# A fused cosine attention and gated MLP on one core: attention visits of three events in three rotating PSUM slots, AV of a quad in one burst, and inverse norms by Newton steps on VectorE

## The chip, the core and the metric

The kernel runs on one core of a Trainium2 chip. The metric is the device time of one execution in microseconds (us); lower is better. The engines are named as in the profile: PE is TensorE (matmul), PEld its weight loads, ACT is ScalarE, DVE is VectorE, POOL is GpSimd, SP is SyncE, which here only issues transfers.

## The reference

```python
q_n = q / (norm(q, axis=-1) + 1e-6)          # q, k, v: 8 batches, 12 heads, 448 tokens, 64 wide
k_n = k / (norm(k, axis=-1) + 1e-6)
scores = q_n @ k_n.T / tau                   # tau = 0.1
attn = exp(scores - max);  attn = attn / (sum(attn) + 1e-9)
x = (attn @ v), heads side by side           # 3584 tokens x 768
h = x @ w_in                                 # 768 x 2048
g = h * cos(h)
out = g @ w_out                              # 2048 x 768
```

## The kernel before

Four heads of one batch are a **quad**; there are 24 quads (three per batch), numbered 0 to 23. A quad's keys come in NJ = 7 blocks of 64. One block's **score event** (`scores`, L551) is four matmuls of 64*64 quarters of the array into two neighbouring PSUM banks, and one ACT exponential E (L567) of 128x896 that empties them. One block's **AV event** (`attend`, L570) is four 64*64 matmuls that add E times V into banks X and Y (4 and 5); after seven of them DVE copies the pair to `AVs` (L586).

The sums of the exponentials are taken by `sums` (L630) for rounds of quads, [3], [4,5], [6,7] and so on: 28 matmuls with a 0/1 matrix into a spare bank, ACT's logarithm and exponential (L649, L651), a small store to DRAM from ACT's queue (L652), four loads from there that spread the reciprocals over the partitions (R, L658, on SP's queue), and a product `xT = AVs * R` on POOL (L662; for quad 5 on DVE).

The inverse norms of a quad come from `inverse` (L461). POOL squares Q and K (L450), DVE sums each 64 (L454), ACT takes logarithm and exponential for the root (L480, L483). For quads up to 7 DVE adds 1e-6 (L486) and takes the reciprocal (L489); from quad 8 two more ACT instructions do that (L491, L493). POOL then scales Q and K (L501), and SP's queue transposes them (`turn`, L539).

The MLP runs by batch c = 0 to 7. **M1** (L670 to L696) is 96 matmuls of 128x448 in eight pairs of banks, and for each pair ACT, DVE, ACT, DVE in turn (L689, L691, L693, L695) make g. **M2** (`m2`, L698) is 96 matmuls of 128x384 for even c and 128 for odd c, 16 to an item, in banks 6 and 7 in turn; DVE copies a finished item out (L722). A few last f blocks of the first two items are put off, since they need the last pairs of g.

The first three quads run alone. After that each batch c is a stage: M1, then M2 with attention of later quads between its matmuls. `QUADS` gives the quads per stage: 5, 4, 3, 3, 3, 3, 0, 0. In a stage `group` is the unit: one score, the AV events of the group before, one more score (groups of 2, 2, 2 and 1 blocks per quad), and then `fill` of some M2 matmuls. Score events use two pairs of banks in turn (0,1 and 2,3). A group is a change of PE from whole-array matmuls to quarter-array ones and back; I call it a **visit**. The AVs of a stage's last group run inside the next M1 (`flush_av`, L739).

All instructions of an engine are put in order by `Planner` (L22), which plays the kernel through with estimated durations; PE keeps the order written down, the other engines take what is ready and most urgent, where `lead` makes an instruction more urgent by so many us. On the chip each engine then works strictly in that order and waits on semaphores. A DVE or ACT instruction that needs the result of an earlier one of its own engine waits for it by semaphore as well.

Of the kernel before, what the change touches and what calls it, by code (L numbers as in the profile page):

```python
# [271 lines left out]
def bass_cosine_attention__then__act_gcu_kernel(  # L272
# [31 lines left out]
    NE, NV, NA = 17, 4, 4  # L304
# [17 lines left out]
    Zs = ring("Zs", 2, [128, S], F32)  # L322
# [105 lines left out]
    H, NLEAD, FAST = 2 * NJ, 5.0, 7  # L428
# [31 lines left out]

    def inverse(qd, w0, w1, part=ALL[0], after=()):  # L461
# [17 lines left out]
        lead = NLEAD * (qd > FIRST + 1)  # L479
        act("exp", 0.12, lambda e: e.activation(z, t, ACT.Ln, bias=1e-30, scale=1.0), r=cells("n2"), w=cells("nrm"),  # L480
            after=after, lead=lead)
# [3 lines left out]
        if 0 < qd <= FAST:  # L485
            op("dve", 0.13, lambda e: e.tensor_reduce(out=o, in_=both, axis=AX.X, op=ALU.add), r=cells("nrm") + ["eps"],  # L486
               w=cells("rr"), lead=lead)
            yield
            op("dve", 0.27, lambda e: e.reciprocal(o, o), r=cells("rr"), w=cells("rr"), lead=lead)  # L489
# [61 lines left out]
    def scores(g):  # L551
# [3 lines left out]
        u, bs, es = qd % 2, 2 * (g % 2), g % NE  # L555
# [14 lines left out]
    def attend(g):  # L570
# [13 lines left out]
        if j == NJ - 1 and qd >= FIRST:  # L584
            sl = qd % NA
            op("dve", 1.01, lambda e: e.tensor_copy(AVs[sl].ap(), two(X)), r=pair(X), w=[("AV", sl)])  # L586

    Z, LEAD = 6, 15.0

    def spread(qd, j0, j1):  # L590
# [14 lines left out]
        if j1 < NJ:  # L605
            return
        summed.add(qd)
        act("exp", 0.815, lambda e: e.activation(ar[s].ap(), two(Z), ACT.Ln, bias=0.0, scale=1.0), r=pair(Z), w=[("ar", s)])
        act("exp", 0.83, lambda e: e.activation(ar[s].ap(), ar[s].ap(), ACT.Exp, bias=0.0, scale=-1.0),  # L609
            r=[("ar", s)], w=[("ar", s)])  # L610

    def scale_x(qd):
        b, c0, s = qd // QB, 2 * (qd % QB), qd % 3
        op("dve", 1.01, lambda e: e.tensor_tensor(xT[b % 2].ap()[:, c0:c0 + 2, :], two(X), ar[s].ap(), ALU.mult),
           r=pair(X) + [("ar", s)], w=[("x", b % 2, qd % QB)])
# [12 lines left out]
    rounds, spared = [0], []  # L628

    def sums(quads, bk):  # L630
# [3 lines left out]
        z = n % 2  # L634
# [3 lines left out]
        def mm(e):  # L638
# [9 lines left out]
        zz = Zs[z].ap()[0:32 * np_, :]  # L648
        act("exp", 0.44, lambda e: e.activation(zz, bank(bk, S, 0, 32 * np_), ACT.Ln, bias=0.0, scale=1.0),  # L649
            r=whole(bk), w=[("Zs", z)], lead=LEAD)  # L650
        act("exp", 0.47, lambda e: e.activation(zz, zz, ACT.Exp, bias=0.0, scale=-1.0), r=[("Zs", z)], w=[("Zs", z)], lead=LEAD)  # L651
        op("act", 0.6, lambda e: e.dma_start(rscr.ap()[8 * n:8 * n + rows, :], Zs[z].ap()[0:32 * np_:16, :]),  # L652
           r=[("Zs", z)], w=[("rs", n)], dma=("rs", z), moves=0.05, lead=LEAD)
        for i, qd in enumerate(quads):
            u, sl, b = qd % 2, qd % NA, qd // QB
            for r in range(2):
# [5 lines left out]
            op("dve" if late else "pool", 1.02 if late else 2.04, lambda e, u=u, sl=sl, b=b, c0=c0: e.tensor_tensor(  # L662
                xT[b % 2].ap()[:, c0:c0 + 2, :], AVs[sl].ap(), R[u].ap(), ALU.mult),
                r=[("AV", sl), ("R", u, 0), ("R", u, 1)], w=[("x", b % 2, qd % QB)], lead=LEAD)
# [18 lines left out]
    def m1(c, pr, bk):  # L683
        s = pairs[0] % 3
        pairs[0] += 1
        col = S * (c % 2)
        bs = pair(bk)

        op("act", 0.815, lambda e: e.activation(ar[s].ap().bitcast(I32), two(bk), ACT.Identity, bias=0.25, scale=INV2PI),  # L689
           r=bs, w=[("ar", s)])  # L690
        op("dve", 1.005, lambda e: e.scalar_tensor_tensor(ar[s].ap(), ar[s].ap().bitcast(I32), -2.0 * math.pi, two(bk),  # L691
                                                          ALU.mult, ALU.add), r=bs + [("ar", s)], w=[("ar", s)])
        act("sin", 0.86, lambda e: e.activation(ar[s].ap(), ar[s].ap(), ACT.Sin, bias=GUARD * math.pi / 2.0, scale=GUARD),  # L693
            r=[("ar", s)], w=[("ar", s)])
        op("dve", 1.01, lambda e: e.tensor_tensor(gT.ap()[:, 2 * pr:2 * pr + 2, col:col + S], two(bk), ar[s].ap(), ALU.mult),  # L695
           r=bs + [("ar", s)], w=[("g", c % 2, 2 * pr), ("g", c % 2, 2 * pr + 1)])  # L696
# [35 lines left out]
    W, MOST = (1, 1), 9  # L732
    ROUNDS = [[FIRST]] + [[i, i + 1] for i in range(FIRST + 1, NQ, 2)]
    E1, E2 = NNB - 6, NNB - 4
    due = []
    last_group = []
    cur = [7]

    def flush_av():  # L739
        while last_group:  # L740
            g = last_group.pop(0)
            attend(g)
            qd, j = divmod(g, NJ)
            if j == NJ - 1 and NV <= qd + NV < NQ:
                load_v(qd + NV)

    def now():
        return [[o for o in P.ops if o.eng == "pe"][-1]]
# [5 lines left out]
    def group(steps):  # L754
        qd, j = divmod(steps[0], NJ)
        if j == 0:
            begin(qd)
        scores(steps[0])
        flush_av()
        for g in steps[1:]:  # L760
            scores(g)
        last_group.extend(steps)
        if FIRST < qd < NQ - 3 and j == 0:
            norm_a(qd + 3, [o for o in P.ops if o.eng == "dve"][-1:])
        if qd + 2 < NQ and j == NJ - 1:
            turn(qd + 2)
            if FIRST < qd < NQ - 4:
                load_qk(qd + 4)
        if j == 0:
            due.extend(r for r in ROUNDS if r[-1] == qd - 1)  # L770

    def groups_of(qd):
        g = NJ * qd
        return [range(g + i, g + min(i + 2, NJ)) for i in range(0, NJ, 2)]
# [141 lines left out]
    done = FIRST  # L916
    for c in range(B):
        last = 2 * ((NJ * done - 1) % 2)
        free = 2 - last
        if c == 0:  # L920
            at_bank = free, last, 6, X, free, 6, last, X
        elif c < B - 1:
            at_bank = free, 6, last, X, 6, free, last, X
        else:
            at_bank = 2 * (6, free, last, X)
        banks = (6, 7, free) if c >= B - 2 else (6, 7)
# [4 lines left out]
        for pr in range(NNB // 2):  # L931
            m1_part(c, pr, at_bank[pr], order if pr < early else (0, 1), late if pr < early else 0, NKC)
            m1(c, pr, at_bank[pr])
            if pr == 1:
                flush_av()
        if c == 0:
            transpose(FIRST, 0, free)
            transpose(FIRST, 1, free + 1)
# [6 lines left out]
        cuts = (0, E1, E2, E2 + 2, NNB)  # L945
        ahead = 2 if len(banks) == 2 else 3
        items[0:ahead * NNB] = [(*work[i], f) for a, b in zip(cuts, cuts[1:]) for i in range(ahead) for f in range(a, b)]
        at = [0]
        bank_of = {}

        def fill(n):
            n = min(n, len(items) - at[0])
            while n > 0:
                t, h, f0 = items[at[0]]
                if len(banks) == 3:
                    if due and at[0] >= E1:
                        sums(due.pop(0), free + 1)
                elif due and len(bank_of) != 1 and at[0] >= 2 * NNB and 2 <= f0 <= 13:
                    sums(due.pop(0), 13 - cur[0])
                f1 = f0  # L960
                while n > 0 and f1 < NNB and items[at[0]:at[0] + 1] == [(t, h, f1)]:
# [3 lines left out]
                    if due and f1 == 2:  # L965
# [5 lines left out]

        new = done + QUADS[c]
        todo = [steps for qd in range(done, new) for steps in groups_of(qd)]
        more = new > done
        done = new
        if todo:
            fill(2 * (E2 if c else E1))
        for i, steps in enumerate(todo):
            if c == 0 and i == 1:
                spared.extend([x([o for o in P.ops if o.eng == "dve"][-1:]) for x in adds])  # L980
                norm_b(FIRST + 2, after=[o for o in P.ops if o.chain][-1:])
            group(steps)
            left = len(items) - at[0]
            share = [W[len(x) & 1] for x in todo[i:]]
            fill(2 * (NNB - E2) + 3 * len(due) if i == 0 else min(MOST, -(-left * share[0] // sum(share))))
        if more and done == NQ:
            flush_av()
            due.extend(r for r in ROUNDS if r[-1] == NQ - 1)
# [37 lines left out]
```

## Time and profile before

| what | value |
|---|---|
| median of 3 runs | 441.71 us (440.83 to 442.9) |
| profiled execution, its own time | 441.8 us |
| its span in the profile | 439.6 us |
| granted TensorE clock, mean | 0.992 of full |
| PE busy | 420.1 us, 3544 matmuls |
| ACT busy | 315.3 us |
| DVE busy | 254.7 us |
| POOL busy | 211.2 us |

The chain of work that ended last gives the starts of M1 in each stage: 38.71, 100.28, 158.54, 208.02, 259.47, 309.11, 360.88 and 396.47 us; M2 of the last stage ends at 435.71 us.

A page or a view is read so: a timeline line gives the start, the time from the start to the end of a run of like instructions, engine, source line, and how long the engine sat idle before and for whom. The windows view gives each engine's busy time in a stretch. A matmul's row holds its way through the array, so rows overlap; what a matmul costs is the distance of starts. Over 24 M2 matmuls in a row that is 0.1625 us each (3.90 us in the chain), over 96 of M1 0.190 us (18.25 us), and an event of four quarter-array matmuls takes 0.19 us.

### The profile page before, as it was taken

How to read it: one execution, taken by the hardware profiler on the slowest of the kernel's cores; microseconds unless marked ns; L12 is line 12 of the kernel's file. 1: busy time of each engine (PE TensorE's matmuls, PEld its weight loads, DVE VectorE, ACT ScalarE, POOL GpSimd, SP SyncE). 2: the span in 40 equal slices, each digit the busy share in tenths (PEclk: the TensorE clock that was granted, in tenths of full speed). 3: DMA queues.
4: the chain of work that ended last, by engine and by line, in shares of the span. 5: the costliest groups of instructions: out<-in, count | busy, mean ns of one | idle time of the engine just before them, and what ended most of it. 6: DMA issues, size and time to landing. Idle time of an engine off the chain costs nothing.

```text
span 439.6 us, 8369 instructions
## 1 busy us (share of the span) xinstructions
PE 420.1 (96%) x3544; PEld 204.6 (47%) x3544; DVE 254.7 (58%) x300; ACT 315.3 (72%) x434; POOL 211.2 (48%) x145
## 2 busy tenths in 40 slices
PE   5989999988999999999999999999999999999996
PEld 5444543324544345434554444434454445555553
DVE  4674995347863449823696419923585237825931
ACT  4798789896788877788688667888678666815700
POOL 3878727869167694376637682148633120030000
PEclk9699999999999999999999999999999999999999
DMA  7999996999919969188933994075912611051022
GB/s 253 233 251 227 261 196 92 233 223 208 146 41 240 240 172 213 37 206 123 265 89 80 241 210 141 1 171 150 259 35 48 154 43 30 0 159 36 1 71 73
DMA packets 70941, 64.34 MB, mean 146 GB/s; under 512 B 40100, under 2 KB 63224, under 8 KB 70904
## 3 DMA queue, kind: packets, MB, share of 16 engines
q1 hardware_dynamic: 57824, 51.30, 46.6%
q0 software_dynamic: 12288, 11.80, 18.2%
q10 hardware_dynamic: 792, 0.71, 0.5%
q8 instruction: 28, 0.46, 0.4%
q14 instruction: 9, 0.07, 0.1%
HBM read 55.25 MB, written 11.16 MB: 151 GB/s over the span
## 4 chain that ended last, share of the span: by engine, by line
PE 83%; ACT 9%; DVE 3%; issue 2%; POOL 2%; ACTq 1%; POOLq 0%
PE PS L676 33%; PE PS L704 31%; PE PS L560 7%; PE PS L577 6%; ACT E L567 6%; PE PS L642 4%; DVE n L454 1%; ACT Zs L651 1%; ACT Zs L649 1%; ACTq L652 1%; PE PS L599 1%; PE PS L623 1%; POOL xT L662 0%; DVE gT L695 0%; ACT ar L609 0%
## 5 line engine op out<-in xcount | busy, mean ns | idle before, releaser
L704 PE MATMUL PS<-W,gT 128*128 128x384 bf16 x896 | 163.4, 327 | 1.1 <-DVE osb L722 1.0
L567 ACT ACTIVATE E<-PS 128x896 bf16<-128x896 f32 x168 | 144.8, 916 | 27.0 <-PE PS L560 23.8
L676 PE MATMUL PS<-xT,W 128*128 128x448 bf16 x768 | 147.7, 353 | 1.2 <-POOL xT L662 1.2
L704 PEld LDWEIGHTS PS<-W,gT 128*128 128x128 bf16 x896 | 80.1, 98 | 80.7 <-issue 29.0
L676 PEld LDWEIGHTS PS<-xT,W 128*128 128x128 bf16 x768 | 74.3, 98 | 72.0 <-POOL xT L662 1.6
L689 ACT ACTIVATE ar<-PS 128x896 int32<-128x896 f32 x64 | 58.2, 910 | 45.1 <-PE PS L676 45.1
L691 DVE SCALAR_TENSOR_TENSOR ar<-ar,PS 128x896 f32<-128x896 int32 x64 | 69.2, 1083 | 29.0 <-ACT ar L689 29.0
L722 DVE COPY osb<-PS 128x384 f32<-128x384 f32 x54 | 29.2, 554 | 86.6 <-PE PS L704 86.5
L662 POOL TENSOR_TENSOR xT<-AVs,R 128x896 bf16<-128x896 f32 x20 | 41.4, 2088 | 67.5 <-DMA R<-rscr 67.4
L695 DVE TENSOR_TENSOR gT<-PS,ar 128x896 bf16<-128x896 f32 x64 | 69.6, 1088 | 1.5 <-ACT ar L693 1.0
L693 ACT ACTIVATE ar<-ar 128x896 f32<-128x896 f32 x64 | 60.6, 946 | 13.1 <-DVE ar L691 13.1
L560 PE MATMUL PS<-qT,kT 64*64 64x448 bf16 x672 | 62.1, 368 | 4.9 <-ACT E L567 4.0
L450 POOL TENSOR_TENSOR sqq<-Qf 128x896 bf16<-128x896 f32 x21 | 35.3, 1679 | 49.3 <-DVE n L454 40.9
L577 PE MATMUL PS<-E,Vb 64*64 64x448 bf16 x672 | 50.4, 353 | 2.1 <-ACT E L567 1.8
L501 POOL TENSOR_TENSOR Qn<-Qf,rr 128x896 bf16<-128x896 f32 x21 | 35.4, 1687 | 29.6 <-ACT rr L493 25.1
L450 POOL TENSOR_TENSOR sqk<-Kf 128x896 bf16<-128x896 f32 (+1 forms) x22 | 36.5, 1659 | 25.9 <-DVE n L454 17.9
L586 DVE COPY AVs<-PS 128x896 f32<-128x896 f32 x21 | 22.8, 1087 | 29.6 <-PE PS L577 29.6
L501 POOL TENSOR_TENSOR Kn<-Kf,rr 128x896 bf16<-128x896 f32 (+1 forms) x22 | 37.5, 1705 | 0.5 <-DVE Qn L501 0.5
L560 PEld LDWEIGHTS PS<-qT,kT 64*64 64x64 bf16 x672 | 18.6, 105 | 38.4 <-issue 15.6
L454 DVE TENSOR_REDUCE n<-sqq 128x14 f32<-128x896 bf16 (+2 forms) x24 | 24.9, 1037 | 5.8 <-POOL sqq L450 5.7
L454 DVE TENSOR_REDUCE n<-sqk 128x14 f32<-128x896 bf16 (+2 forms) x24 | 25.0, 1040 | 5.4 <-POOL sqk L450 5.4
L577 PEld LDWEIGHTS PS<-E,Vb 64*64 64x64 bf16 x672 | 19.3, 106 | 17.5 <-ACT E L567 10.6
(53 smaller groups left out, 175.9 us busy)
## 6 DMA issues: line engine op xcount, KB each, us to landing
Qf<-in_q_dram SPq DMA_DIRECT2D x24, 448.0 KB, 6.0
out_dram<-osb SPq DMA_DIRECT2D x54, 192.0 KB, 3.6
Kf<-in_k_dram SPq DMA_DIRECT2D x23, 448.0 KB, 7.2
R<-rscr SPq DMA_DIRECT2D x42, 224.0 KB, 4.2
Vb<-in_v_dram POOLq DMA_DIRECT2D x24, 224.0 KB, 6.7
W<-in_moe_w_in_dram POOLq DMA_DIRECT2D x4, 768.0 KB, 18.3
W<-in_moe_w_out_dram POOLq DMA_DIRECT2D x4, 768.0 KB, 31.9
Kf<-in_k_dram ACTq DMA_DIRECT2D x1, 320.0 KB, 6.2
```

The source lines that it names most:

```text
L450: op(eng, (1.68 if eng == "pool" else 1.05) * n, lambda e: e.tensor_tensor(dst, src, src, ALU.mult), r=cut(nm + "f", s, part), w=at, after ...
L454: return op("dve", 0.07 + 0.95 * n, lambda e: e.tensor_reduce(out=n2[u].ap()[:, H * w:H * w + H] if part == ALL[0] else jr(n2[u], w, part) ...
L501: lambda e: e.tensor_tensor(n[u].ap()[:, j0:j1].rearrange("p j r d -> p r j d"), f[s].ap()[:, :, j0:j1], rb, ALU.mult),
L560: ins = e.matmul(bank(bs + r, S, 64 * a, 64 * a + 64), kT[u].ap()[64 * r:64 * r + 64, j, a, :], qT[u].ap()[64 * r:64 * r + 64, :, a, :], s ...
L567: act("exp", 0.875, lambda e: e.activation(E[es].ap(), two(bs), ACT.Exp, bias=0.0, scale=INV_TAU), r=pair(bs), w=[("E", es)], chain="E")
L577: ins = e.matmul(bank((X, Y)[a], S, 64 * r, 64 * r + 64), Vb[vs].ap()[64 * a:64 * a + 64, r, j, :], E[es].ap()[64 * a:64 * a + 64, r, :], ...
L676: ins = e.matmul(bank(bk + i2), W1.ap()[:, i, 128 * nb:128 * nb + 128], xT[c % 2].ap()[:, i, :], start=(i == 0), stop=(i == NKC - 1))
L689: op("act", 0.815, lambda e: e.activation(ar[s].ap().bitcast(I32), two(bk), ACT.Identity, bias=0.25, scale=INV2PI), r=bs, w=[("ar", s)])
L691: op("dve", 1.005, lambda e: e.scalar_tensor_tensor(ar[s].ap(), ar[s].ap().bitcast(I32), -2.0 * math.pi, two(bk), ALU.mult, ALU.add), r=bs ...
L693: act("sin", 0.86, lambda e: e.activation(ar[s].ap(), ar[s].ap(), ACT.Sin, bias=GUARD * math.pi / 2.0, scale=GUARD), r=[("ar", s)], w=[("a ...
L695: op("dve", 1.01, lambda e: e.tensor_tensor(gT.ap()[:, 2 * pr:2 * pr + 2, col:col + S], two(bk), ar[s].ap(), ALU.mult), r=bs + [("ar", s)] ...
L704: ins = e.matmul(bank(bk, HW), gT.ap()[:, f, col:col + 128], W2.ap()[:, f, HW * h:HW * h + HW], start=(f == 0), stop=(f == NNB - 1))
```

## The change

It has six parts.

1. `visits_of` and `visit` take the place of `group`. A visit has three score events. A finished quad's AV is no longer spread over the groups: `gather` does all its seven AV events in one burst of 28 matmuls, put third in the visit after the one in which the quad's last score stood. Score events and bursts share three slots of two banks (0 to 5), in turn; a burst's slot is emptied by DVE's copy to `AVs`.
2. `pace` sets the number of M2 matmuls after each visit from a small model of PE, ACT and the slots; 14 are wished after the last visit of a stage.
3. From quad 3 on, `inverse` gives way to `newton`: 13 small DVE instructions in a dependent chain (a bit-trick start, three Newton steps of three instructions, product with the squared norm, plus 1e-6, reciprocal). No ACT instruction is left in it.
4. The last pair of each M1 is worked on bank by bank: twice four instructions of half the size.
5. The put-off M2 blocks: the first item is finished before the second one's last six blocks, and sums may stand in the middle of items (f 2 to 11).
6. Rings: E from 17 to 18 buffers, one Zs in place of two; `product` waits in program order until a quad's burst is written.

```diff
-    NE, NV, NA = 17, 4, 4
+    NE, NV, NA = 18, 4, 4
...
+    def newton(qd, lead, after):
+        u = qd % 2
+        a, y = n2[u].ap(), rr[u].ap()
+        s, t = (bass.AP(nrm[0], H * 2 * i, [[4 * H, 128], [1, 2 * H]]) for i in range(2))
...
+        step(lambda e: e.tensor_scalar(y.bitcast(I32), a.bitcast(I32), -0.5, float(0x5F3759DF), ALU.mult, ALU.add),
+             n2s, rrs, after=after)
+        yield
+        for _ in range(3):
+            step(lambda e: e.scalar_tensor_tensor(s, a, BIG, y, ALU.min, ALU.mult), n2s + rrs, ss)
+            step(lambda e: e.scalar_tensor_tensor(t, s, -0.5, y, ALU.mult, ALU.mult), ss + rrs, ts)
+            step(lambda e: e.scalar_tensor_tensor(y, t, 1.5, y, ALU.add, ALU.mult), ts + rrs, rrs)
+            yield
+        step(lambda e: e.scalar_tensor_tensor(s, a, BIG, y, ALU.min, ALU.mult), n2s + rrs, ss)
+        step(lambda e: e.tensor_scalar(t, s, 1e-6, None, ALU.add), ss, ts)
+        step(lambda e: e.reciprocal(y, t), ts, rrs, 0.2)
...
+        if qd >= FIRST:
+            yield from newton(qd, lead, after)
+            return
...
-        u, bs, es = qd % 2, 2 * (g % 2), g % NE
+        u, bs, es = qd % 2, 2 * (g % 2 if slot is None else slot), g % NE
...
+    def gather(qd, slot):
+        vs, sl, bs = qd % NV, qd % NA, 2 * slot
+        es = [(NJ * qd + j) % NE for j in range(NJ)]
+        def mm(e):
+            for j in range(NJ):
+                for a in range(2):
+                    for r in range(2):
+                        ins = e.matmul(bank(bs + a, S, 64 * r, 64 * r + 64),
+                                       Vb[vs].ap()[64 * a:64 * a + 64, r, j, :],
+                                       E[es[j]].ap()[64 * a:64 * a + 64, r, :],
+                                       start=(j == 0), stop=(j == NJ - 1))
+            return ins
+        op("pe", 0.188 * NJ, mm, r=[("E", i) for i in es] + [("V", vs)], w=pair(bs), mode="q")
+        op("dve", 1.01, lambda e: e.tensor_copy(AVs[sl].ap(), two(bs)), r=pair(bs), w=[("AV", sl)])
...
+        for part in ((0, 1), (1, 2)) if pr == NNB // 2 - 1 else ((0, 2),):
+            some(*part)
...
+    def visits_of(quads):
+        steps = [(qd, j) for qd in quads for j in range(NJ)]
+        out, late = [], []
+        while steps:
+            what, steps = steps[:3], steps[3:]
+            now_, later = late, []
+            for p, (qd, j) in enumerate(what):
+                if j == NJ - 1:
+                    (later if p else now_).extend(x for x in ROUNDS if x[-1] == qd)
+            ended = [qd for qd, j in what if j == NJ - 1]
+            if owed:
+                what.insert(2, (owed.pop(0), None))
+            owed.extend(ended)
+            out.append((what, now_))
+            late = later
+        return out, late
+    def slot():
+        events[0] += 1
+        return (events[0] - 1) % 3
+    def visit(what):
+        for qd, j in what:
+            if j == 0:
+                begin(qd)
+            if j is None:
+                gather(qd, slot())
+            else:
+                scores(NJ * qd + j, slot())
...
-        cuts = (0, E1, E2, E2 + 2, NNB)
-        items[0:ahead * NNB] = [(*work[i], f) for a, b in zip(cuts, cuts[1:]) for i in range(ahead) for f in range(a, b)]
+        cuts = [(i, 0, E1) for i in range(ahead)] + [(i, E1, E0) for i in range(ahead - 1)]
+        cuts += [(i, E0, NNB) for i in range(ahead - 1)] + [(ahead - 1, E1, NNB)]
+        items[0:ahead * NNB] = [(*work[i], f) for i, a, b in cuts for f in range(a, b)]
...
+        def can_sum(p):
+            if ahead == 3:
+                return p >= E1
+            return ahead * NNB <= p < len(items) and 2 <= items[p][2] <= 11
...
+        if visits:
+            fill(2 * E1 + (4 if c else 0))
+            fills = pace(visits, len(items) - at[0], 14)
+            for i, (what, rounds_here) in enumerate(visits):
...
+                visit(what)
+                due.extend(rounds_here)
+                n = fills[i]
+                while due and not any(can_sum(p) for p in range(at[0], at[0] + n)):
+                    n += 1
+                fill(n)
+            if done == NQ:
+                gather(owed.pop(0), slot())
+                due.extend(left)
+            else:
+                carried = left
```

More of the change, by code (lines that the diff above doesn't have):

```diff
@@ L549, in bass_cosine_attention__then__act_gcu_kernel, with scores @@
     holds = {}
-    def scores(g):
+    def scores(g, slot=None):
         qd, j = divmod(g, NJ)
@@ L583, in attend, with ars @@
         op("pe", 0.19, mm, r=[("E", es), ("V", vs)], w=pair(X), mode="q")
-        if j == NJ - 1 and qd >= FIRST:
-            sl = qd % NA
-            op("dve", 1.01, lambda e: e.tensor_copy(AVs[sl].ap(), two(X)), r=pair(X), w=[("AV", sl)])
+    def gather(qd, slot):
[12 more added lines that the diff above has]
+        op("dve", 1.01, lambda e: e.tensor_copy(AVs[sl].ap(), two(bs)), r=pair(bs), w=[("AV", sl)])
+        gathered.add(qd)
+        if qd in products:
+            products.pop(qd)()
+        if qd + NV < NQ:
+            load_v(qd + NV)
     Z, LEAD = 6, 15.0
+    def ars(s, i0=0, i1=2):
+        return [("ar", s, i) for i in range(i0, i1)]
     def spread(qd, j0, j1):
@@ L954, in fill @@
                 t, h, f0 = items[at[0]]
[L955 to L959, printed above, removed]
+                if due and can_sum(at[0]):
+                    sums(due.pop(0), 13 - cur[0] if ahead == 2 else n0 + 1)
                 f1 = f0
@@ L970, in fill @@
                 m2(t, h, f0, f1, bank_of[t, h])
[L972 to L988, printed above, removed]
+        visits, left = visits_of(range(done, done + QUADS[c]))
+        if carried and visits:
+            visits[0][1].extend(carried)
+            carried = []
+        done += QUADS[c]
+        if visits:
+            fill(2 * E1 + (4 if c else 0))
+            fills = pace(visits, len(items) - at[0], 14)
+            for i, (what, rounds_here) in enumerate(visits):
+                if c == 0 and i == 1:
+                    spared.extend([x([o for o in P.ops if o.eng == "dve"][-1:]) for x in adds])
+                    norm_b(FIRST + 2, after=[o for o in P.ops if o.chain][-1:])
+                visit(what)
+                due.extend(rounds_here)
+                n = fills[i]
+                while due and not any(can_sum(p) for p in range(at[0], at[0] + n)):
+                    n += 1
+                fill(n)
+            if done == NQ:
+                gather(owed.pop(0), slot())
+                due.extend(left)
+            else:
+                carried = left
         fill(len(items))
```

179 lines of the change are left out of this document (110 added, 69 removed).

## The prediction

> **What bounds the kernel now.** I read the page first, then the chain that ended last, then the attention stages by the windows view, then their timelines.
>
> ```profile
> PE 420.1 (96%) x3544; PEld 204.6 (47%) x3544; DVE 254.7 (58%) x300; ACT 315.3 (72%) x434; POOL 211.2 (48%) x145
> ...
> PE 83%; ACT 9%; DVE 3%; issue 2%; POOL 2%; ACTq 1%; POOLq 0%
> ```
>
> PE carries the chain. So I add up PE's own work by stage, with the costs in the table of before: M1 18.25 us, M2 0.1625 a matmul, 0.19 an event, 1.45 a round of sums. What is left over is the visit:
>
> ```profile
> 191.13 1.15 PE L704 MATMUL PS<-W,gT 128*128 128x384 bf16 x6
> 192.21 0.38 PE L560 MATMUL PS<-qT,kT 64*64 64x448 bf16 x4
> 192.43 0.36 PE L577 MATMUL PS<-E,Vb 64*64 64x448 bf16 x4
> 192.62 0.36 PE L560 MATMUL PS<-qT,kT 64*64 64x448 bf16 x4
> 192.91 1.15 PE L704 MATMUL PS<-W,gT 128*128 128x384 bf16 x6
> ```
>
> From 191.13 to 192.91 are 1.78 us, of which six matmuls take 0.975 and three events 0.57. The rest, 0.235 us, is the change to quarter-array matmuls and back; the visit at 194.93 to 196.89, with four events, leaves 0.225, which I take. There are 84 groups and 6 flushed ends, 90 visits. Work against length by stage (from one start of M1 to the next), with 20, 17, 13, 13, 13, 13 visits: c=0 55.2 of 61.57, c=1 56.4 of 58.26, c=2 47.7 of 49.48, c=3 51.4 of 51.45, c=4 47.7 of 49.64, c=5 51.4 of 51.77. So PE waits 6.3 us in c=0, 6.2 in c=1 to 5 together, nearly all of it in c=1, 2 and 4. What it waits for there:
>
> ```profile
> 183.26 0.50 PE L704 MATMUL PS<-W,gT 128*128 128x384 bf16 x2 [0.33 <-DVE osb L722]
> ...
> 188.05 0.38 PE L560 MATMUL PS<-qT,kT 64*64 64x448 bf16 x4 [0.59 <-ACT E L567]
> ...
> 188.86 0.38 PE L577 MATMUL PS<-E,Vb 64*64 64x448 bf16 x4 [0.24 <-ACT E L567]
> ```
>
> The third item finds no free bank after the first two end together, and scores find both slots unread, because ACT has just done the sums' two instructions and norms. In c=0 ACT itself is full:
>
> ```profile
> 61.60:100.28 38.68, 34.39 (x390) 12.73 (x387) 20.06 (x28) 33.93 (x53) 27.87 (x19) 1.00 0.93 186
> ...
> 181.00:208.00 27.00, 25.85 (x294) 10.87 (x294) 11.23 (x14) 22.69 (x37) 18.79 (x12) 1.00 0.68 143
> ```
>
> (columns: stretch, length, busy PE, PEld, DVE, ACT, POOL). And M1 of c=1 waits in the end for the products of quads 4 and 5:
>
> ```profile
> 86.80 0.58 ACT L651 ACTIVATE Zs<-Zs 128x448 f32<-128x448 f32 x1
> 87.40 0.57 ACTq L652 DMA_DIRECT2D rscr<-Zs  x1
> ```
> ```profile
> 93.28 2.86 SPq L658 DMA_DIRECT2D R<-rscr  x4
> ```
> ```profile
> 98.15 2.08 POOL L662 TENSOR_TENSOR xT<-AVs,R 128x896 bf16<-128x896 f32 x1
> 100.19 2.53 POOL L501 TENSOR_TENSOR Kn<-Kf,rr 128x896 bf16<-128x896 f32 x1
> 102.68 1.68 POOL L501 TENSOR_TENSOR Qn<-Qf,rr 128x896 bf16<-128x896 f32 x1
> ```
> ```profile
> 99.75 1.43 DVE L662 TENSOR_TENSOR xT<-AVs,R 128x896 bf16<-128x896 f32 x1
> ```
>
> From the end of the sums (86.1) to M1 (100.28) are 14.1 us, 5.3 of them the store's landing (87.97 to 93.28); in c=2 the same step took 1.2 (187.03 to 188.24).
>
> **The change, part by part.** The base is the profiled execution, 441.8 us (span 439.6 and 2.2 around it); the median, 441.71, is 0.1 off, so nothing is converted.
>
> *Visits.* Steps in threes give 12, 10, 7, 7, 7, 7 visits and one last burst, 51 in all. Events and sums stay as many. Outside c=0 31 visits go: 31 x 0.225 = **-7.0 us**, on PE's path.
>
> *Waits of c=1 to 5 (6.2 us).* Exponentials follow each other every 0.866 us (two in 1.73). In c=2 and 4 ACT must do 21 of them and two rounds of sums at 1.7 (0.57 + 0.58 + 0.57): 21.6 us, without the norms (four instructions 0.26 apart, 3.1 us for three quads) that it has now. PE needs 72 x 0.1625 + 42 x 0.19 + 2.9 + 7 x 0.225 = 24.2 us from the first visit on. ACT stands idle some 2.3 us behind the first visit, which is followed by at least 11 matmuls and the carried round of sums. 23.9 against 24.2 is too tight to be free: I leave 0.9 us of waiting in c=2 and 4 each, 0.5 in c=1 (27.6 against 32.7), 0.3 in c=3 and 5 each (19.9 against 27.9). The wait for osb (0.63 us from 182.63 to 183.26, again in c=1 and 4) goes, as the first item now ends six matmuls earlier. 6.2 - 2.9 = **-3.3 us** (0 to -6). The burst's slot must be copied by DVE (1.09 us) before it serves again three events later, a visit with its filling; that fits unless DVE is late, priced below.
>
> *Stage c=0.* ACT: 35 x 0.866 + 3.4 = 33.7 us from the first exponential at 61.63. The sums of [4,5] need 21 exponentials and one round, 81.5; then comes the burst (1.32), a score and the sums, so they end near 84.6, not 86.1: -1.5. Behind them stand the same 14.1 us; POOL's wait for ACT's rr (Qn at 93.22 came 4.3 us late) goes, the landing may shrink from 5.3 towards 1.2: to -4.5. Against it, quads 3 and 4 now put 26 small instructions on DVE at 41.2, where 2.4 us are free before M1's first pair (now 1.0 used): up to +2.0 on M1, some of it won back, as DVE needs 2.1 us a pair and PE gives one every 2.28. I take **-2.0 us** (-4.5 to +0.6).
>
> *Newton on DVE.* Nearest rows:
>
> ```profile
> 65.00 0.20 DVE L486 TENSOR_REDUCE rr<-nrm 128x28 f32<-128x56 f32 x1
> 65.23 0.33 DVE L489 RECIPROCAL rr<-rr 128x28 f32<-128x28 f32 x1
> ```
>
> A dependent step is bounded by 0.15 (the shortest L486) and 0.33; I take 0.20, the small one that is no division: 12 x 0.20 + 0.33 = 2.7 us a quad, 57 us in all for 21 quads, beside 254.7. As sheer load it fits: DVE was busy 11.2 of 27 us in c=2. [...]
>
> The price is order: DVE's copies, which free banks, queue behind the chain. There are 77 of them (56 osb, 21 AVs) in 397 us, one per 5.15. A bank is wanted again after an item, 16 x 0.1625, and a visit of 0.8: 3.4 us, less the copy's 0.56, leaves 2.85 of slack. A chain of 2.7 hides. But the one DVE product of two SBUF tiles shown above started at 99.75 inside a POOL product, and ended at 101.18, 0.95 after that one did (100.23); POOL's next took 2.53 in place of 1.68. So they took turns. Ten of Newton's steps have two SBUF tiles. If a chain meets one POOL instruction it lasts 4.4 us; a copy that comes at any time in it loses (1.55 x 1.55 / 2) / 4.4 = 0.27 us on PE, x 4.4 / 5.15 copies, x 18 quads (the stages c=0 to 4, where POOL is busy over 60% of the time): **+4.2 us** (0 to +18).
>
> *M1's halves, rings.* Nothing: eight stages get four short instructions more, DVE's last product ends 4.3 us after M1 (181.3 against 177.0), and its first user comes 24 matmuls and a visit behind M1, at 4.7; were it late, that is 0.1 to 0.3 us a stage.
>
> Sum: -7.0 - 3.3 - 2.0 + 4.2 = -8.1, so 433.7 us.
>
> **Rivals.** *(B) Only the visits pay.* E waits just move into the visits (three slots, the third score waiting for an exponential as the second did), and c=0 stays with its chain of sums, products and transfers. For it: 23.9 against 24.2 above. Then -7.0 + 4.2: 439.0 us.
>
> *(C) Slower: DVE held by POOL.* Each chain meets two POOL instructions, as the squares and the scalings come in pairs (1.68 each), and lasts 6.1 us. A copy then loses (3.25 x 3.25 / 2) / 6.1 = 0.87 us, x 6.1 / 5.15 x 18 = 18.4 us, against -12.3: 447.9 us. It decides from a loss of 12.3 / 18 = 0.68 us a chain. For it: POOL busy 18.8 of 27 us in c=2, and xT pairs of 4.13 us. Against it: POOL's order often has it waiting for the very rr that Newton makes, and then it is idle. [...]
>
> *(D) The burst waits.* It needs its quad's last E, which may be ready only 3.0 us after its visit began (0.4 + 3 x 0.866), while PE is there after 0.8 + 1.65 + 0.4 = 2.85. With ACT behind by the sums that is about 0.35 us, x 21 = 7.4 on top of the forecast: 441.1, no change.
>
> **How the numbers follow.** Forecast 0.52 (427 to 439), B 0.20, C 0.20, D 0.08. The low end, 427, is -7.0 - 3.3 - 4.5 without the DVE price. The range 427 to 447 leaves out 0.05 below and about half of C. A measurement here tells about 0.5% (2.2 us) from no change. Faster: the forecast nearly whole and three quarters of B, 0.67; same: the rest of B and D, 0.11; slower 0.22.
>
> **What would show it.** Visits: 51 runs of score events; 0.225 us beyond their events. ACT: lines of the norms only for quads 0 to 2, and E back to back in c=0. [...] D shows as PE idle ahead of the burst "<-ACT E". The sum of stages c=1 to 5, 260.6 us now, should fall by about 7; if c=0 (61.57) does not fall below 60, the landing or POOL's order there was the bound. I am wrong if DVE's queue costs nothing, or more than 12 us.

## The result and the profile after

The changed kernel takes 473.15 us (median of 4 runs, 468.27 to 474.44) against 442.3 us for the kernel before beside it: 1.069 times as long, 95% interval 1.064 to 1.0739. The forecast was 433.7 us, between 427 and 447: a gain of 8 us was expected, and 31 us were lost.

The page's line of busy times and the engines' shares of the chain that ended last, after:

```profile
PE 422.4 (90%) x3544; PEld 214.6 (46%) x3544; DVE 330.7 (70%) x579; ACT 301.9 (64%) x376; POOL 210.3 (45%) x145
...
PE 50%; DVE 32%; ACT 8%; issue 4%; POOL 4%; DMA 2%; ACTq 0%; SPq 0%; POOLq 0%; DVEq 0%
```

ACT lost 13 us and POOL has the same work. DVE has 279 instructions and 76 us more, and its share of the chain went from 3% to 32%. PE's own waits say the same. This is the waits view of PE, with total us, number and longest:

```profile
PE PS L589 <- DVE AVs L629: 9.4, 4, 3.9
PE PS L769 <- DVE osb L787: 6.5, 4, 2.3
PE PS L733 <- DVE gT L757: 5.6, 4, 3.2
```

With 3.2 us more that the sums wait for osb, DVE's copies of AVs and osb and its product gT are late by 24.7 us. In the kernel before, the view has one such line:

```profile
PE PS L704 <- DVE osb L722: 1.0, 3, 0.3
```

The place of the longest wait, with DVE, POOL and PE in the timeline:

```profile
73.95 1.69 POOL L530 TENSOR_TENSOR Kn<-Kf,rr 128x896 bf16<-128x896 f32 x1
74.77 0.90 DVE L474 TENSOR_SCALAR rr<-n 128x28 int32<-128x28 int32 x1
75.60 1.68 POOL L450 TENSOR_TENSOR sqk<-Kf 128x896 bf16<-128x896 f32 x1
75.71 1.61 DVE L478 SCALAR_TENSOR_TENSOR nrm<-n,rr 128x28 f32<-128x28 f32 x1
...
78.06 0.82 PE L769 MATMUL PS<-W,gT 128*128 128x384 bf16 x4
...
79.92 1.09 DVE L454 TENSOR_REDUCE n<-sqq 128x14 f32<-128x896 bf16 x1
80.93 1.08 DVE L454 TENSOR_REDUCE n<-sqk 128x14 f32<-128x896 bf16 x1
81.92 1.08 DVE L629 COPY AVs<-PS 128x896 f32<-128x896 f32 x1
83.06 0.77 PE L589 MATMUL PS<-qT,kT 64*64 64x448 bf16 x8 [3.86 <-DVE AVs L629]
83.76 1.46 PE L769 MATMUL PS<-W,gT 128*128 128x384 bf16 x4
```

The columns are start, length and, in brackets, the idle time before and what ended it. Two steps that take 0.18 to 0.19 us unhindered take 0.90 and 1.61 here. Each ends within 0.1 us of the POOL instruction that was under way when it began (75.67 and 75.64; 77.32 and 77.28). The chain lasts 5.1 us (to 79.89), two sums of squares follow it (79.92 to 82.01), and the copy that frees the burst's slot stands behind all of them, although the burst had ended at 77.9. PE waits 3.86 us. Then four M2 matmuls take 1.46 us; four of the same kind, ahead of that wait at 78.06, took 0.82.

Over the whole run 24 of the 273 Newton steps are over 0.4 us (7 in L474, 5 in L478, 6 each in L479 and L480). All 24 end 0.03 to 0.05 us after a POOL instruction that ran beside them. The rows sum to 84.2 us where 273 unlocked steps would be 53.8: 30.4 us of DVE time spent waiting inside instructions, 1.45 us a quad.

To see where the time went I count every kernel the same way: from one start of M1 to the next, less the products (the prediction's costs a matmul and an event) and less 0.225 us a visit. What is left is waiting, together with what matmuls lose at a lower granted clock (0.57 behind the wait of 3.86 us above; last section). (Before comes to 7.2 us in c=0 and 5.7 in c=1 to 5; the prediction has 6.3 and 6.2, as it put 0.8 us more of work into c=0.) "Visits only" is the first experiment, "paced" the ninth.

| waiting, us | c=0 | c=1 | c=2 | c=3 | c=4 | c=5 | sum | visits x 0.225 |
|---|---|---|---|---|---|---|---|---|
| before | 7.2 | 1.7 | 1.8 | 0.1 | 2.0 | 0.1 | 12.9 | 90: 20.3 |
| after | 22.1 | 11.4 | 6.4 | 7.0 | 6.9 | 1.7 | 55.5 | 51: 11.5 |
| visits only | 11.5 | 5.3 | 1.7 | 0.9 | 5.4 | 0.9 | 25.7 | 51: 11.5 |
| paced | 11.3 | 4.1 | 2.2 | 1.0 | 3.4 | 1.0 | 23.0 | 51: 11.5 |

So the switching did fall by 8.8 us, and the waiting rose by 42.6. The difference, 33.8, less an earlier first M1 (1.3) and 0.5 in c=6 and 7, is the 32 us between the two spans (471.6 and 439.6).

### The profile page after: what moved, and what is told of

Its sections match the earlier page's. It is cut to its first block, busy times and chain, and to the rows that moved or that the text cites. A ratio compares the mean times of both kernels' runs of the same rounds, so it can differ in the third digit from the quotient of the medians.

```text
span 471.6 us, 8611 instructions
## 1 busy us (share of the span) xinstructions
PE 422.4 (90%) x3544; PEld 214.6 (46%) x3544; DVE 330.7 (70%) x579; ACT 301.9 (64%) x376; POOL 210.3 (45%) x145
## 4 chain that ended last, share of the span: by engine, by line
PE 50%; DVE 32%; ACT 8%; issue 4%; POOL 4%; DMA 2%; ACTq 0%; SPq 0%; POOLq 0%; DVEq 0%
PE PS L733 20%; PE PS L769 18%; DVE gT L757 6%; DVE ar L752 6%; ACT E L596 4%; DVE n L454 4%; PE PS L589 4%; DVE nrm L479 3%; DVE nrm L478 3%; PE PS L622 3%; PE PS L692 3%; DVE rr L480 3%; DVE rr L474 2%; DVE osb L787 1%; DVE AVs L629 1%
## 5 line engine op out<-in xcount | busy, mean ns | idle before, releaser
L733 PE MATMUL PS<-xT,W 128*128 128x448 bf16 x768 | 150.4, 357 | 8.9 <-DVE gT L757 5.6
L769 PEld LDWEIGHTS PS<-W,gT 128*128 128x128 bf16 x896 | 84.0, 99 | 81.3 <-issue 23.1
L751 ACT ACTIVATE ar<-PS 128x896 int32<-128x896 f32 (+1 forms) x72 | 59.1, 827 | 55.6 <-PE PS L733 55.6
L752 DVE SCALAR_TENSOR_TENSOR ar<-ar,PS 128x896 f32<-128x896 int32 (+1 forms) x72 | 69.8, 976 | 19.0 <-ACT ar L751 19.0
L754 ACT ACTIVATE ar<-ar 128x896 f32<-128x896 f32 (+1 forms) x72 | 61.8, 864 | 22.9 <-DVE ar L752 21.8
L757 DVE TENSOR_TENSOR gT<-PS,ar 128x896 bf16<-128x896 f32 (+1 forms) x72 | 70.2, 982 | 1.7 <-ACT ar L754 1.0
L589 PE MATMUL PS<-qT,kT 64*64 64x448 bf16 x672 | 53.5, 378 | 16.4 <-DVE AVs L629 9.4
L629 DVE COPY AVs<-PS 128x896 f32<-128x896 f32 x21 | 22.6, 1077 | 21.8 <-PE PS L622 21.8
L589 PEld LDWEIGHTS PS<-qT,kT 64*64 64x64 bf16 x672 | 16.0, 107 | 45.1 <-ACT E L596 15.5
L622 PE MATMUL PS<-E,Vb 64*64 64x448 bf16 x588 | 31.9, 354 | 1.6 <-ACT E L596 1.4
L692 PE MATMUL PS<-E,sel 128*32 128x448 bf16 x294 | 17.9, 375 | 5.9 <-DVE osb L787 3.2
```

Source lines behind the costliest of these rows:

```text
L589: ins = e.matmul(bank(bs + r, S, 64 * a, 64 * a + 64), kT[u].ap()[64 * r:64 * r + 64, j, a, :], qT[u].ap()[64 * r:64 * r + 64, :, a, :], s ...
L622: ins = e.matmul(bank(bs + a, S, 64 * r, 64 * r + 64), Vb[vs].ap()[64 * a:64 * a + 64, r, j, :], E[es[j]].ap()[64 * a:64 * a + 64, r, :], ...
L733: ins = e.matmul(bank(bk + i2), W1.ap()[:, i, 128 * nb:128 * nb + 128], xT[c % 2].ap()[:, i, :], start=(i == 0), stop=(i == NKC - 1))
L751: op("act", 0.225 + 0.295 * n, lambda e: e.activation(ai, src, ACT.Identity, bias=0.25, scale=INV2PI), r=bs, w=at)
L752: op("dve", 0.07 + 0.47 * n, lambda e: e.scalar_tensor_tensor(a, ai, -2.0 * math.pi, src, ALU.mult, ALU.add), r=bs + at, w=at)
L754: act("sin", 0.225 + 0.32 * n, lambda e: e.activation(a, a, ACT.Sin, bias=GUARD * math.pi / 2.0, scale=GUARD), r=at, w=at)
```

## The experiments

Three theories. LOCK: the long steps, each held until a POOL instruction beside it ends (this I call the lock), are the loss. LOAD: thirteen more instructions in DVE's order are, lock or not. VISITS: the new visits themselves cost time. "Before" is the kernel before on the same chip.

| run | kernel | us | before | ratio, 95% interval |
|---|---|---|---|---|
| 1 | after, norms on ACT as before | 445.25 | 441.63 | 1.0045 to 1.0101 |
| 2 | before, with Newton | 475.12 | 441.63 | 1.0702 to 1.0819 |
| 3 | after, one-input steps | 451.4 | 441.63 | 1.0154 to 1.0283 |
| 4 | run 1, M1's last pair whole | 445.5 | 441.63 | 1.0048 to 1.0103 |
| 5 | after, norms by one reciprocal | 442.8 | 442.37 | 0.999 to 1.0033 |
| 6 | before, norms by one reciprocal | 447.88 | 442.37 | 1.0116 to 1.0147 |
| 7 | run 1, sums later | 445.36 | 442.37 | 1.0058 to 1.0085 |
| 8 | run 7, fewer norms on ACT | 443.93 | 442.37 | 1.0026 to 1.0057 |
| 9 | run 8, paced anew | 442.67 | 442.13 | 0.9988 to 1.003 |
| 10 | run 3, first step as in after | 456.36 | 442.13 | 1.0293 to 1.0356 |
| 11 | run 3, first step 1.46 us longer | 477.97 | 442.13 | 1.0781 to 1.0847 |
| 12 | run 9, quads 4,4,4,3,3,3 | 466.83 | 441.96 | 1.0534 to 1.0618 |
| 13 | before, quads 4,4,4,3,3,3 | 460.11 | 441.96 | 1.0381 to 1.0441 |
| 14 | run 9, half of each E | 436.93 | 442.27 | 0.9873 to 0.994 |
| 15 | before, half of each E | 438.67 | 442.27 | 0.9912 to 0.9955 |

### Which part costs the time: runs 1, 2 and 4

Run 1 takes Newton out; norms are made as before.

```diff
-        if qd >= FIRST:
-            assert part == ALL[0] and (w0, w1) == (0, 2)
-            yield from newton(qd, lead, after)
-            return
...
-        if qd:
+        if 0 < qd <= 7:
```

> The changed kernel with part 3 undone: inverse norms from ACT and DVE as before (two ACT, two DVE instructions up to quad 7, four ACT instructions after that); visits, bursts, pace, halves, rings stay. Theory LOCK (a Newton step with two SBUF tiles waits for the POOL instruction under way, and DVE's queue with it): 430 to 438 us, against 473 with the change and 442 before. Theory LOAD (thirteen more instructions a quad in DVE's queue cost by their number and place, lock or not): the same, 430 to 438. Theory VISITS (the three slots and the bursts are what costs): 455 or more.

Run 2 is the reverse: the kernel before with `newton` and its call added, nothing else.

> The kernel before with part 3 alone: Newton steps on DVE from quad 3 on, everything else as before. LOCK and LOAD: 455 to 475 us, rows of Newton steps of 1 us and more where POOL is at work. VISITS: 440 to 446, since ACT is even relieved.

Run 4 is run 1 with M1's last pair whole again (`for part in ((0, 2),)`).

> As the run without Newton steps, and the last pair of each M1 worked on whole (part 4 undone too). If the halves are worth anything, this is 0.5 to 3 us slower than that run, through the last products of M1 and their M2 matmuls; by the prediction's price of nothing, within 1 us.

Newton costs 27.9 us in the new visits (473.15 against 445.25) and 33.5 us in the old ones (475.12 against 441.63). VISITS falls as the cause of the loss. But run 1 is 3.6 us above the kernel before, not 12 below it, and above the 430 to 438 us that LOCK and LOAD gave: the other half of the forecast failed too. The halves are worth 0.25 us, nothing.

### Lock or load: runs 3, 10 and 11

Run 3 keeps the number and the order of a chain's steps but gives the first twelve one SBUF input each; the root is left out.

```diff
+        def one(out, src, r, w, **kw):
+            step(lambda e: e.tensor_reduce(out=out, in_=pairs_of(src), axis=AX.X, op=ALU.max), r, w, **kw)
...
-            step(lambda e: e.scalar_tensor_tensor(s, a, BIG, y, ALU.min, ALU.mult), n2s + rrs, ss)
...
+            one(s, y, n2s + rrs, ss)
```

> The changed kernel, but the first twelve of the thirteen small DVE instructions of a chain are maxima over pairs of equal numbers (128x28 from 128x56, one SBUF tile read, about 0.20 us each as L486 before); same number, same dependence, same order on every engine. It leaves out the root: Q and K are scaled by the reciprocal of the squared norm, so the numbers differ, the work after it doesn't. LOCK: 430 to 442 us, and no small row on DVE above 0.35 us. LOAD: 465 to 475, as the change. VISITS: 465 to 475.

One of DVE's rows of run 3 by form (busy us, mean ns, idle before):

```profile
L478 DVE TENSOR_REDUCE nrm<-nrm 128x28 f32<-128x56 f32 x84 | 17.7, 210 | 2.7
```

and the same view of the changed kernel:

```profile
L479 DVE SCALAR_TENSOR_TENSOR nrm<-nrm,rr 128x28 f32<-128x28 f32 x63 | 20.9, 332 | 2.0
```

A reduction is the slower instruction unlocked, 0.21 against 0.19 us, yet its mean is 210 ns and none of its 252 rows is over 0.214 us, whereas this two-input step has a mean of 332. The time falls by 21.8 us, and the rows of the chains sum to 59.8 us in place of 84.2. What is left of Newton, 6.2 us over run 1, is the load of 21 chains that last 3.3 us where nothing comes between their steps (0.25 from step to step, the reciprocal 0.33). So 451.4 us lies between the two forecasts, nearer to LOCK: most of the loss is the lock, the rest is load.

Run 10 puts the changed kernel's first step, integers from one tile, back into run 3.

> The third run's kernel (12 of the 13 steps with one SBUF input; the root is left out) with the first step of each chain as the changed kernel has it: multiply and add on the integers, one SBUF input, 128x28. In the changed kernel 7 of 21 such steps took over 0.4 us. If the one-input integer step is held by a GpSimd instruction as the two-input ones are, some 5 to 9 of the 21 are over 0.4 us again, and the time is 455 to 460 us (a quarter to a third of the 21.8 us that the lock cost). If it was long only by what stood around it, all are under 0.25 us and the time is that of the third run, 451.4 us, within 1.5.

```profile
L480 DVE TENSOR_SCALAR rr<-n 128x28 int32<-128x28 int32 x21 | 9.8, 471 | 6.2 <-ACT E L602 5.8
```

Six of the 21 are over 0.4 us (up to 1.69) and end within 0.05 us of a POOL instruction, all reductions stay at 0.21, and the time rises by 5.0 us. So a step with one SBUF input was held as well. Why this one was and no reduction was, the runs do not show.

Run 11 tells what a held step costs whom. The first step of run 3 reads 52 copies of each element, so that it takes 1.67 us, without any lock.

```diff
+        many = bass.AP(a.tensor, a.offset, [*a.ap, [0, 52]])
+        step(lambda e: e.tensor_reduce(out=y, in_=many, axis=AX.X, op=ALU.max), n2s, rrs, after=after)
```

> The third run's kernel (one SBUF input in 12 of 13 steps; the root is left out) with the first step of each chain made 1.4 us longer by more elements (52 copies of each, still one SBUF input), so that each chain holds VectorE as long as the chains of the changed kernel did on the mean (30 us in 21 chains), and no lock is in it. Theory BLOCK: what the lock costs is the time in which VectorE does nothing else, so this kernel comes back to 465 to 480 us. Theory MOMENT: the lock hurts because it strikes when GpSimd is at work, in the dense stretches, and the same time spread over all chains costs less than half: 452 to 461 us.

BLOCK holds, MOMENT falls: 21 x 1.46 = 30.7 us more of DVE time cost 26.6 us. The long step is the same every time, and PE's waits of run 11 are of the changed kernel's kinds and sizes:

```profile
L481 DVE TENSOR_REDUCE rr<-n 128x28 f32<-128x1456 f32 x21 | 35.0, 1669 | 8.6 <-ACT E L602 8.2
```
```profile
PE PS L775 <- DVE osb L793: 8.9, 5, 2.7
PE PS L595 <- DVE AVs L635: 7.4, 7, 2.3
```

So the time for which the lock stops DVE's queue is enough to explain its price. The changed kernel's chains are busy 24.4 us longer than run 3's and cost 21.8 us more, 0.89 us for each; without any lock run 11 pays 0.87.

### Where the visits' gain went: runs 5 to 9 and 12 to 15

In run 1 the visit itself costs what the prediction took. In c=3:

```profile
249.64 0.76 PE L585 MATMUL PS<-qT,kT 64*64 64x448 bf16 x12
250.34 2.29 PE L765 MATMUL PS<-W,gT 128*128 128x384 bf16 x13
252.55 0.57 PE L585 MATMUL PS<-qT,kT 64*64 64x448 bf16 x8
```

2.91 us from visit to visit, less three events (0.57) and 13 matmuls (2.11), are 0.23. But PE waits for ACT, 12.2 us in the first four rows here, of run 1, against 5.8 in the last two, of the kernel before:

```profile
PE PS L585 <- ACT E L592: 4.4, 13, 0.5
PE PS L688 <- ACT E L592: 2.7, 3, 1.4
PE PS L618 <- ACT E L592: 2.6, 5, 0.9
PE PS L585 <- ACT nrm L505: 2.5, 1, 2.5
```
```profile
PE PS L560 <- ACT E L567: 4.0, 8, 0.8
PE PS L577 <- ACT E L567: 1.8, 7, 0.4
```

Two theories of that. NORM: the norm chains left on ACT delay it. PLACE: the new visits wait for what they themselves place (three scores on ACT at once, the sums right behind the last score). In runs 5 and 6 one reciprocal on DVE stands for all norms from quad 3, the fourth (the root and the 1e-6 are left out).

```diff
+        if qd >= FIRST:
+            op("dve", 0.33, lambda e: e.reciprocal(rr[u].ap(), n2[u].ap()), ...)
+            return
```

> The changed kernel with the inverse norms from quad four on by one VectorE reciprocal of the sum of squares (the root and the 1e-6 are left out): neither ScalarE nor VectorE carries a chain any more. Without Newton the visits came to 445.25 us against 441.6 before, although the switching of 90 visits fell to that of 51 (8.8 us less). Theory NORM: the chains that are left on ScalarE (two to four short activations a quad, queued among the exponentials) hold the norms, the transposes and the exponentials up, and the denser visits feel it; then this kernel is 8 to 9 us under the kernel before with the same free norms (the sixth run), 431 to 436 us. Theory PLACE: the visits of three wait for their own exponentials (slots, bursts, sums placed right behind the last score), whatever the norms do; then this kernel is 2 to 5 us above the sixth run, 442 to 445 us.

> The kernel before with the same one reciprocal on VectorE for the inverse norms from quad four on (the root and the 1e-6 are left out). It is the base for the fifth run and the price of the norms in the old visits. Both theories: 438 to 442 us, since the old stages have little wait outside the first (1.5 us a stage at most) and VectorE has room for 21 instructions of 0.33 us. A value under 437 says that ScalarE's norm chains cost the old kernel too.

Neither: the difference is 5.1 us, and it is not the visits' alone. Run 6, forecast at 438 to 442 us, rose by 5.5 us, mostly because M1 of c=1 waited longer for the products of its x (3.48 us for POOL's, 2.09 for DVE's, against 1.18 before). The lock is in that too: DVE's product, 1.08 us in the changed kernel, began beside a POOL instruction, lasted through that one and the next two, and ended 0.95 us after the third (103.83):

```profile
99.54 5.24 DVE L666 TENSOR_TENSOR xT<-AVs,R 128x896 bf16<-128x896 f32 x1
102.14 1.69 POOL L505 TENSOR_TENSOR Kn<-Kf,rr 128x896 bf16<-128x896 f32 x1
```

From the start of c=2 to the end of c=5 the two are level: 202.4 and 202.8 us.

Run 7 takes the sums in the middle of a filling instead of right behind the visit; run 8 leaves ACT two instructions a norm for all quads but the first.

```diff
+                n = fills[i]
+                if rounds_here:
+                    fill(n // 2)
+                    n -= n // 2
                 due.extend(rounds_here)
-                n = fills[i]
```

> The changed kernel with ScalarE's norms again (as in the first run), and with each sum round taken in the middle of the product matmuls that follow its visit instead of right behind the visit. Theory PLACE: the waits that the sums have for the last exponential in the trace of the first run (1.41, 0.64 and 0.64 us, and others of that size in stages two to six) go, 3 to 5 us: 440 to 442.5 us. Theory NORM: the sums move a wait to the next visit, 444.5 to 446 us.

> The seventh run's kernel, with the norms of all quads but the first by two activations on ScalarE and two one-input instructions on VectorE (a reduction over the pair and a reciprocal), where the kernel before does so up to quad seven only: 14 quads get two activations less and two VectorE instructions more. PLACE: no more than 0.5 us from the seventh run. NORM: 1 to 4 us under it, since two of four links of each late chain leave ScalarE's queue.

Run 7 gained nothing, a miss for PLACE: c=1 and c=4 lost 1.1 us of waiting each, c=0 and c=2 took 1.6 on. Run 8 gained 1.4, at the low end of NORM. Run 9 mends two places of the order.

```diff
-            fills = pace(visits, len(items) - at[0], 14)
+            fills = pace(visits, len(items) - at[0], 14, 1.0 if c else 4.0)
...
-            return ahead * NNB <= p < len(items) and 2 <= items[p][2] <= 11
+            return ahead * NNB <= p < len(items) and 4 <= items[p][2] <= 13
```

(the new last argument of `pace` is the start value of `act_`)

> The eighth run's kernel with two edits to where the visits stand. The pacing of the first stage assumes that ScalarE still has 4 us to do when the first visit comes (it assumed 1 us), so that more product matmuls stand ahead of the third visit, whose scores waited 2.55 us in the eighth run while the next sums then ran 1 us slow; and a sum round is taken not before the fifth product of an item, so that the copy of the item before has its bank free (waits of 0.33 to 0.55 us behind osb). Theory PLACE (the saved switching was given back in waits that the order sets): 2 to 4 us under the eighth run, 440 to 442 us, no slower than the kernel before. Rival: the first stage is bound by ScalarE, and the wait only moves to its later visits: within 0.7 us of the eighth run.

442.67 us, 1.3 under run 8 and as fast as the kernel before (the interval holds 1). Of the new versions that leave nothing out it is the fastest, and it does not beat the old one. The long wait at the third visit of c=0 broke up, but the eight waits of run 9 for ACT in c=0 still add up to 5.2 us.

Runs 12 and 13 move a quad out of c=0 by `QUADS = [4, 4, 4, 3, 3, 3, 0, 0]`, in the new visits and in the old.

> The ninth run's kernel with the quads of the stages as 4, 4, 4, 3, 3, 3 instead of 5, 4, 3, 3, 3, 3: seven exponentials (0.83 us each on ScalarE, 5.8 us) and their scores go from the first stage to the third. In the ninth run the first stage has 11.3 us that are neither products nor switching, and its scores and bursts wait for ScalarE in eight places of 0.38 to 1.22 us, while the third has 2.2. Theory ACT-BOUND (in the first stage ScalarE sets the end, so that fewer switches on TensorE buy nothing there): the waits of the first stage go, the third stage takes some, and the time falls by 2 to 4 us, 438.5 to 441 us. Rival, PLACE: what is left are the waits that any visit of three brings with it (three exponentials behind three scores), wherever it stands: within 1 us of the ninth run, 441.7 to 443.7 us.

> The kernel before with the same quads, 4, 4, 4, 3, 3, 3: the base for the twelfth run. ACT-BOUND: the first stage of the kernel before has 7.2 us of such rest with 20 visits, so it gains too, 1 to 3 us, 439 to 441 us, and the twelfth run is 0 to 2 us under it. PLACE: 441.5 to 443 us.

Both are slower, by 24 and 18 us, and answer nothing about the visits: M1 of c=1 and M1 of c=2 now wait for x, 6.3 to 8.5 us each time. In run 13:

```profile
101.11 2.08 POOL L662 TENSOR_TENSOR xT<-AVs,R 128x896 bf16<-128x896 f32 x1
103.25 1.30 PE L676 MATMUL PS<-xT,W 128*128 128x448 bf16 x3 [8.45 <-POOL xT L662]
```

With fewer quads in c=0, the last product that M1 of c=1 needs falls near the stage's end, here behind two scalings and two squares on POOL (94.55 to 101.16). So runs 14 and 15 keep every order and shorten the exponentials: from quad 3, the fourth, half of each is left out, 128x448 in place of 128x896.

> The ninth run's kernel (quads 5, 4, 3, 3, 3, 3) with each exponential from quad four on taken over half of its columns, 128x448 in place of 128x896 (half of the exponentials are left out and old values stand in their place): 147 instructions of ScalarE some 0.37 us shorter, by the ratio that its other instructions of these two widths have. Nothing else and no order changes. Theory ACT-BOUND: the waits of visits, bursts and slots for ScalarE go, and the new visits are worth what the count of visits says: 5 to 9 us under the fifteenth run. Theory PLACE: the new visits lose as much to other waits (osb, transposes, norms, the product at a stage's end) as they save: within 2.5 us of the fifteenth run on either side.

> The kernel before with the same halved exponentials from quad four on (half of them are left out): the base for the fourteenth run. ACT-BOUND: the old visits wait for ScalarE less (2.2 us of such waits over 0.3 us in the first stage, 1.2 in the others), so 437 to 441 us. PLACE: the same.

The new visits are now 1.7 us faster than the old by the medians, 1.3 by the means; single executions scatter over 2.6 and 1.9 us, so that this gain itself is not clear of noise. ACT-BOUND, which asked for 5 to 9, falls as the whole cause all the same; of the 8.8 us, ACT's exponentials hold back some 2, as far as that scatter allows a number (run 14 against 15, beside run 9 against before, +0.5). PLACE's range holds: counted as in the table, run 14 still waits 18.0 us and run 15 10.9. What PE waits for in run 14 is mixed:

```profile
PE PS L585 <- DMA kT<-Kn: 3.5, 2, 1.9
PE PS L585 <- ACT E L593: 3.3, 6, 0.9
PE PS L585 <- ACT nrm L508: 1.6, 1, 1.6
PE PS L766 <- DVE osb L784: 1.4, 3, 0.7
```

The wait of 1.9 us, for the transposed keys of quad 20, can be followed. POOL had scaled them at 284.17, but on SP's queue the transposes stand behind the four loads of a round of sums (285.79 to 288.18). Counted from the start of c=4, the keys' transpose is issued after 34.8 us and lands 5.0 us later; in run 15 it is issued after 33.8 us and lands 5.5 us later. PE is there after 38.1 us in run 14 and after 40.6 in run 15, where it does not wait. So the denser visits ask for the keys earlier than the order of the transfers brings them. How much of the 8.8 us the other waits take, one by one, was not settled.

## Why the prediction was wrong

- **Newton on DVE, +4.2 us forecast, 27.9 measured: the step that failed is the price of a chain that outlasts the slack.** The parts were nearly right. The unlocked chain was to last 2.7 us and lasts 3.0 (steps 0.22 apart, the reciprocal 0.33). One long step a chain was assumed, and there are 24 in 21 chains. A slack near 2.85 us fits run 3, whose chains of 3.3 us cost 0.3 each. But a copy was to come at any moment of the chain and lose a part of the 1.55 us beyond the slack, 0.27 us on the mean. That treats DVE as otherwise empty. The timeline shows the next DVE instructions already queued behind the chain, and most of its excess goes on to PE: 0.87 us for each us added in run 11, 0.89 for the lock, 5.0 us for 5.5 in run 10. Charged whole, the prediction's own numbers give 18 x 1.55 = 27.9 us; that this is the measured figure to the digit is luck, as 21 chains lost time to the lock, 1.45 us each on the mean. The prediction also counted only osb and AVs; gT made PE wait 5.6 us more.
- **Rival C** had the right mechanism and sign, but through two POOL instructions a chain; its 447.9 us used the same formula and fell 25 us short. One was enough. I gave it 0.20.
- **Visits, -7.0 us: right in size** (0.23 us in run 1, 90 to 51 visits) and not seen in the time, since waits grew by 12.8 us beside them (table, visits only).
- **Waits of c=1 to 5, -3.3 us: wrong in sign.** They went from 5.7 to 14.2 us in run 1. "23.9 against 24.2" was a sum over a stage. Within it three scores reach ACT together, and bursts and sums need the last E of their quad; run 9 with more room and less ACT work still has 11.7. The sums were misplaced too: by their matmuls c=1 has three rounds and c=2 one, not two each, and in run 1 c=1 waits 3.6 us more than before, c=2 no more. (The stages' five differences, as printed, sum to 6.0 us, not 6.2.)
- **Stage c=0, -2.0 us: wrong.** 61.6 us became 63.0 without Newton and 73.6 with it. The small DVE instructions of quads 3 and 4 in M1, priced at up to +2.0, held gT back in two places by 3.17 and 0.58 us, and M1 of c=1 waited 3.27 for POOL's last product.
- **Rival D**: in run 1 five bursts waited for E, three of them in c=0, 0.94 us at most and 2.6 in all: 0.12 a quad, not 0.35. **M1's halves**: nothing, as forecast (run 4).
- **Rival B**, waits that move into the visits, is nearest to what the visits did; even it counted -7.0 as gained.

## What to carry to other kernels

Before moving a chain to an engine that is 58% busy, ask what that engine's queue holds at that moment: where others wait on each of its copies, time beyond the slack can cost most of its length on the critical engine (here 0.87 us for each in run 11, 0.89 for the lock), and not that length times a chance. The small VectorE steps here, beside a GpSimd that was busy 45% of the span, cost not their own 0.19 us alone: 24 of 273 took 0.42 to 2.12 us and ended with a GpSimd instruction of 1.7 to 2.1 us that they met; run 8, whose reductions and reciprocals read one tile each, has no row over 0.33 us among them. A saving in switches counts only if the engine that feeds the fuller visits has its results ready, so sum the slack by visit, not by stage.

## What the runs showed of the hardware

The lock was seen the other way round too. In run 9 DVE's product from two tiles is under way when POOL's next scaling begins:

```profile
102.51 1.75 DVE L710 TENSOR_TENSOR xT<-AVs,R 128x896 bf16<-128x896 f32 x1
103.27 2.54 POOL L526 TENSOR_TENSOR Kn<-Kf,rr 128x896 bf16<-128x896 f32 x1
```

Scalings take 1.68 us elsewhere; this one took 0.86 more.

In some places PE lost more than the length of a wait. In run 1 PE stood 2.49 us, and the 14 sum matmuls after it took 2.80 us; in run 9, without that wait, the same 14 took 1.50:

```profile
68.62 0.76 PE L585 MATMUL PS<-qT,kT 64*64 64x448 bf16 x8 [2.49 <-ACT nrm L505]
69.31 2.80 PE L688 MATMUL PS<-E,sel 128*32 128x448 bf16 x14
```

The granted clock by the windows view was 0.54 from 68.6 to 72 us in run 1, and in the changed kernel 0.57 from 83 to 87 us, behind the wait of 3.86 us. A lower clock does not follow every wait: behind one of 2.12 us at 302.66 in run 1 it stayed at 1.00. In the changed kernel it was 0.50 in six stretches, 23.8 us in all, with PE busy in 21.8 of them, and in the kernel before 1.00 from 36 to 439 us. As matmuls take about twice as long there (2.80 against 1.50, 1.46 against 0.82), some 11 of the 55.5 us in the table are slow matmuls, by this estimate, and not waits. Which waits a lower clock follows, the runs do not settle.
